# Reordering the start of a fused adaLN, linear-attention and SwiGLU kernel: the last q tile between the shift products, another order of the first norms, another bank rotation

## The chip, the cores and the metric

The kernel runs on one core of one Trainium2 chip. TensorE (PE) multiplies, VectorE (DVE) and ScalarE (ACT) work on its results and on SBUF, GpSimd (POOL) does a few small operations, and SyncE (SP) issues the DMAs. The metric is the device time of one execution in microseconds (us). The time before is 828.32 us, the median of three runs (827.97 to 828.67).

## The reference, cut to what matters

One transformer block over a sequence of 2048 tokens of width 1024, in bf16, with its norms modulated by a condition vector:

```python
def _A_ref(x, wqkv, wo):                      # linear attention, 32 heads of 32
    q, k, v = split(x @ wqkv)
    phi = lambda t: jnp.where(t > 0, t + 1, jnp.exp(t)) + 1e-06
    pq, pk = (phi(q), phi(k))
    kv = jnp.einsum('bhsd,bhse->bhde', pk, v)
    z = jnp.einsum('bhsd->bhd', pk)
    num = jnp.einsum('bhqd,bhde->bhqe', pq, kv)
    den = jnp.einsum('bhqd,bhd->bhq', pq, z)[..., None] + 1e-06
    return merge_heads(num / den) @ wo

mod = (_silu(c) @ w_mod).reshape(c.shape[0], 6, 1, -1)
sa, ca, ga, sb, cb, gb = mod                  # shift, scale and gate of each half
h = _layernorm(x, axis=-1) * (1 + ca) + sa
x = x + ga * _A_ref(h, A_wqkv, A_wo)
h = _layernorm(x, axis=-1) * (1 + cb) + sb
x = x + gb * _B_ref(h, B_w_gate, B_w_up, B_w_down)   # (silu(h@wg) * (h@wu)) @ wd, width 3584
```

The change touches only the first part: the first layer norm of tokens 0 to 1023, its modulation with `ca` and `sa`, and the q and k products of the first 512 tokens.

## The kernel before

**Order and synchronisation.** Every operation is written once, in program order, through a small recorder (`P.pe`, `P.dve`, `P.act`, `P.pool`, `P.dma`). Each engine executes its own operations strictly in that order. The recorder adds a wait wherever an operation reads or overwrites what another engine or a DMA wrote or still reads. In SBUF it follows byte ranges, so two tiles placed on the same bytes depend on each other. In PSUM it follows whole banks: when an engine touches a bank, it waits for the last operation of every other engine on that bank. All operations are recorded at line 176, so the profile tells them apart by their tiles. There is no planner; the order is written by hand.

**Tokens.** The sequence is cut into 16 tiles of 128 tokens (`st`) and 4 chunks of 512 tokens (`ch`). `XRES` holds x, `HT` holds the normalised, modulated and transposed activations of two chunks (buffer `ch % 2`), eight tiles of 128 features (`dt`) each. `WQK` holds the q and k weights.

**Start (lines 628 to 661).** Tiles 0 and 2 get their mean and variance on VectorE (`bn_stats` twice, `bn_aggr`, `ln1_rstd1`); tiles 1 and 3 get sums on ScalarE (`act_stats`), from which VectorE makes the variance (`msq_neg`, `ve_sums`). POOL raises each variance to -0.5. VectorE normalises each tile in place (`ln1_xn`, `ln1_xn_sum`), and TensorE transposes it into PSUM banks 4 to 7 (`tile_transposes`). `mod_sc` computes columns of the modulation: for each of the columns asked for, eight products with one moving column, into PSUM bank 0. `fin_ca` and `fin_sa` copy the scale (plus 1) and the shift out of bank 0. `warm` issues TensorE products on zeros, which nothing reads. `h0_first` scales a transposed `dt` tile out of PSUM into `HT`; `raw_copy` moves the last four unscaled.

**q of chunk 0 (`q_phase_chunk0`, line 773).** The q products of chunk 0 run while the weights of `w_mod` and `WQK` still arrive. Seven q tiles (`nt` 0 to 6) accumulate in banks 1, 2, 3, 4, 6, 7, 5 at once, over `dt` in passes. The first four `dt` tiles are scaled but not shifted; their shift is added as a bias per output feature. That bias is a product of the shift column and the weights (`bias_mm`), accumulated in bank 0 and copied to `BIASQ` by `bias_fin`. The eighth q tile runs last, in bank 0, after that copy:

```python
for i, dt in enumerate((4, 5, 0, 1, 2, 3, 6, 7)):
    P.pe("matmul", out=PS[:, 0, :], lhsT=WQK[:, dt, 896:1024], rhs=HT[:, 0, dt, :], ...)
```

After it `h0_shift` adds the shift to `dt` 0 to 3 for the k products. `q_phi` computes the exponential and the relu of each q tile on ScalarE with the bias; `q_min` and `q_add` finish phi on VectorE into `PQT`. In between, tiles 4 to 7 (chunk 1) are normalised and transposed by DMA from SP (`th_dma`).

**k of chunk 0 and the later chunks.** `k_group` and `q_group` compute one output tile of 128 features over a whole chunk, eight products, into a bank from `next_bank`, and `phi_evac` evicts it. A k tile takes one exponential on ScalarE into one of four slots of `E1`, then, for two tiles together, a min on VectorE and a `scalar_tensor_tensor` that reads the bank again and writes `PKT` (`phi_flush`). Side work hangs on the groups: `kside[gi]` is recorded behind group `gi` of chunk 0, and `s1`, `s2`, `s3` behind the groups of chunks 1 to 3. The modulation of chunk 1's `HT` (`th_mod`, in halves of 256 tokens: tiles 4 and 5, then 6 and 7) hangs on group 1 of chunk 0. In chunk 1 the side work is the norms of chunk 2 (groups 0 to 2), its modulation, divided between VectorE (even `dt`) and ScalarE (odd `dt`) at groups 9 to 11, and ScalarE's sums of tiles 14 and 15. Chunks run 8 k groups and 8 q groups each.

**Loads.** SP issues all loads in one order: x tiles 0 to 3, the first half of `WCA` (the scale's weights), parts of `WQK`, the second half of `WCA`, more of `WQK`, `WSA` half 1 (the shift's weights), the rest of q's `WQK`, `WSA` half 0 in two pieces, x tiles 4 and 5, k weights, x tiles 6 and 7, k weights, x tiles 8 to 11. Then come the transposing DMAs of tiles 4 to 7 and x tiles 12 to 15.

**The rest** (attention's products, output projection, SwiGLU) runs from about 126 us to the end and isn't touched.

Of the kernel before, what the change touches and what calls it, by code (L numbers as in the profile page):

```python
# [5 lines left out]
FP32 = mybir.dt.float32  # L6
# [256 lines left out]
def bass_adaLN_cond__linear_attn_block__swiglu_ffn__prompt_kernel(  # L263
# [22 lines left out]
    with ExitStack() as es:  # L286
# [6 lines left out]
        def T(name, off, shape, dt):  # L293
            n = 1
            for s_ in shape[1:]:
                n *= s_
            assert off % 32 == 0 and off + n * mybir.dt.size(dt) <= ARENA, (name, off, shape)
            return nc.alloc_sbuf_tensor_at(name, shape, dt, offset=base + off)
# [47 lines left out]
        RL = T("rl", 188 * KB, [128, 4, 512], BF16)  # L346
        E1X = T("e1x", 192 * KB, [128, 4, 512], BF16)
        RLX = T("rlx", 196 * KB, [128, 4, 512], BF16)
        ACC = T("acc", 192 * KB, [128, D], FP32)
        MHL = T("mhl", 196 * KB, [128, 2, D], BF16)  # L350
        MHLT = T("mhlt", 192 * KB, [128, 2 * NDT, 128], BF16)
# [105 lines left out]
        def warm(n=1, bank=2):  # L457
            for _ in range(n):
                P.pe("matmul", out=PS[:, bank, :], lhsT=IDENT[:], rhs=E1[:, 0, :], start=True, stop=True)
# [23 lines left out]
        def ln1_xn(st, c0=0, c1=D):  # L483
            P.dve("tensor_scalar", out=XRES[:, st, c0:c1], in0=XRES[:, st, c0:c1],
                  scalar1=MV[:, st, 0:1], scalar2=RSTD[:, st:st + 1], op0=ALU.subtract, op1=ALU.mult)
# [22 lines left out]
        def mod_sc(w, c0, ms, kts=range(NDT)):  # L508
            for m in ms:
                for kt in kts:  # L510
                    P.pe("matmul", out=PS[:, 0, c0 + m:c0 + m + 1], lhsT=w[:, kt, m * 128:(m + 1) * 128],
                         rhs=SILUC[:, kt:kt + 1], start=mod_first[0], stop=(kt == NDT - 1), skip_group_check=True)
                    mod_first[0] = False

        def fin_ca(m, n):
            P.dve("tensor_scalar", out=MODCOL[:, 0, m:m + n], in0=PS[:, 0, 8 + m:8 + m + n], scalar1=1.0, scalar2=None,
                  op0=ALU.add)

        def fin_sa(m, n, cast=False):
# [42 lines left out]
        def ln1_rstd1(st):  # L562
            P.dve("tensor_scalar", out=VE[:, st:st + 1], in0=MV[:, st, 1:2], scalar1=EPS, scalar2=None, op0=ALU.add)
            P.pool("tensor_tensor", out=RSTD[:, st:st + 1], in0=VE[:, st:st + 1], in1=NEGHALF[:, 0:1], op=ALU.pow)
# [13 lines left out]
        def act_stats(st, passes=(0, 1)):  # L578
            junk0 = HT[:, 1, 0:2, :] if st < 4 else JUNK1[:]
            for i in passes:  # L580
                fn_, sc_, acc_ = ((ACT.Identity, 1.0 / D, SUMX), (ACT.Square, D ** -0.5, SUMSQ))[i]
                P.act("activation", out=junk0, in_=XRES[:, st, :].rearrange("p (a b) -> p a b", a=2),
                      func=fn_, scale=sc_, accum_out=acc_[:, st:st + 1])
# [39 lines left out]
        def ve_sums(st):  # L623
            P.dve("tensor_scalar", out=VE[:, st:st + 1], in0=SUMSQ[:, st:st + 1], scalar1=MV[:, st, 1:2], scalar2=EPS,
                  op0=ALU.add, op1=ALU.add)
            pool_pow(st)

        warm(13, bank=3)
        act_stats(1)
        act_stats(3)  # L630
        for f in s0_:
# [1 line left out]
        ln1_rstd1(0)  # L633
        msq_neg(1)
        s2_[0]()
        ln1_xn(0)
        tile_transposes(0)
        warm(5, bank=3)
        ve_sums(1)
        s2_[1]()  # L640
        s2_[2]()
        ln1_rstd1(2)
        ln1_xn_sum(1)
        tile_transposes(1)
        warm(1, bank=3)
        msq_neg(3)
        ln1_xn(2, 0, 512)
        ve_sums(3)
        ln1_xn(2, 512, D)
        tile_transposes(2)  # L650
        mod_sc(WCA, 8, range(2))
        ln1_xn_sum(3, 0, 512)
        ln1_xn_sum(3, 512, D)
        fin_ca(0, 2)
        tile_transposes(3)
        mod_sc(WCA, 8, range(2, 4))
        h0_first(0, "dve")
        h0_first(1, "dve")
        raw_copy(4, "dve")
# [43 lines left out]
        def next_bank():  # L703
            i = qk_ctr[0]
            qk_ctr[0] += 1
            return (1, 2, 3, 4, 6, 7, 5, 0)[i % 8] if i < 40 else i % 5 + 1

        def q_group(ch, nt):
            buf, bank = ch % 2, next_bank()
# [39 lines left out]
        def mod_row_b(bank, i, dst):  # L749
# [3 lines left out]
            P.wait_for("sp", [wr])  # L753
            P.dma("mdr%d" % i, dst[:], MDR[i].unsqueeze(0).to_broadcast([128, D]))

        def q_slot(nt):
            return (E1, RL) if nt < 4 else (E1X, RLX)

        def q_phi(nt, bank):
            for buf, fn_ in zip(q_slot(nt), (ACT.Exp, ACT.Relu)):  # L760
                P.act("activation", out=buf[:, nt % 4, :], in_=PS[:, bank, :], func=fn_, bias=BIASQ[:, nt:nt + 1])

        def q_min(nts):
            for nt in nts:
                e = q_slot(nt)[0][:, nt % 4, :]
                P.dve("tensor_scalar", out=e, in0=e, scalar1=1.0, scalar2=1e-6, op0=ALU.min, op1=ALU.add)

        def q_add(nts):
            for nt in nts:
                e, r = q_slot(nt)  # L770
                P.dve("tensor_tensor", out=PQT[:, nt, 0:512], in0=r[:, nt % 4, :], in1=e[:, nt % 4, :], op=ALU.add)

        def q_phase_chunk0():
            qb = [1, 2, 3, 4, 6, 7, 5]
            fin_ca(2, 2)
            for dt in (2, 3):
                h0_first(dt, "dve")
            for nts, dts in ((range(3), (0,)), (range(3), (1,)), ((3, 4, 5, 6), (0, 1))):
                for nt in nts:
                    q_part(nt, qb[nt], dts)  # L780
            for nt in range(7):
                if nt == 4:
                    mod_sc(WCA, 8, range(4, 8))
                    fin_ca(4, 4)
                    for dt in (4, 5):
                        h0_scale_only(dt)
                q_part(nt, qb[nt], (2, 3))
            act_stats(4, (0,))
            for nt in range(7):
                if nt == 6:  # L790
                    mod_sc(WSA, 0, range(6, 8))
                    fin_sa(6, 2)
                    for dt in (6, 7):
                        h0_scale(dt)
                q_part(nt, qb[nt], (4, 5))
            mod_sc(WSA, 0, range(4, 6))
            fin_sa(4, 2, True)
            for dt in (4, 5):
                h0_shift(dt)
            for nt in range(7):  # L800
                if nt == 2:
                    bias_mm((4, 5))
                q_part(nt, qb[nt], (6,))
            for nt in range(7):
                if nt == 1:
                    mod_sc(WSA, 0, range(4), range(4))
                if nt == 3:
                    mod_sc(WSA, 0, range(4), range(4, 8))
                    fin_sa(0, 4, True)
                    ln_ops[1][0]()  # L810
                if nt == 5:
                    bias_mm(range(4))
                    bias_fin()
                q_part(nt, qb[nt], (7,))
            ln_ops[1][1]()
            ln_ops[1][2]()
            ln1_rstd1(5)
            for i, dt in enumerate((4, 5, 0, 1, 2, 3, 6, 7)):
                P.pe("matmul", out=PS[:, 0, :], lhsT=WQK[:, dt, 896:1024], rhs=HT[:, 0, dt, :], start=(i == 0),
                     stop=(i == 7))  # L820
            for dt in range(4):
                h0_shift(dt)
            ln1_xn(5)
            th_dma(5)
            for nt in range(2):
                q_phi(nt, qb[nt])
            act_stats(4, (1,))
            for nt in range(2, 8):
                q_phi(nt, qb[nt] if nt < 7 else 0)
            for f in ln_ops[2]:  # L830
                f()
            act_var(4)
            pool_pow(4)
            for f in ln_ops[3]:
                f()
            ln1_rstd2(6)
            ln1_xn_sum(4)
            th_dma(4)
            q_min((0, 1))
            for st in (6, 7):  # L840
                ln1_xn(st)
                th_dma(st)
            q_add((0, 1))
            for nts in ((2, 3), (4, 5)):
                q_min(nts)
                q_add(nts)
            qk_ctr[0] = 0

        def add(d, k, f):
# [2 lines left out]
        kside = {}  # L852
        ln_ops = [ln1_stats_ops(4 + jj) for jj in range(4)]

        for c0 in (0, 256):
            for dt in range(NDT):
                add(kside, 1, lambda dt=dt, c0=c0: th_mod(1, dt, c0, c0 + 256))
        add(kside, 1, lambda: q_min((6, 7)))
        add(kside, 1, lambda: q_add((6, 7)))
        for jj, k in ((0, 3), (1, 4)):  # L860
            add(kside, k, lambda jj=jj: act_stats(10 + jj))
        q_phase_chunk0()
        for st in range(12, 16):
# [384 lines left out]
```

## Time and profile before

| what | value |
|---|---|
| median of three runs | 828.32 us (827.97 to 828.67) |
| the profiled execution | 827.71 us |
| its span, first to last instruction | 826.0 us |
| granted TensorE clock | 1.000 |
| TensorE matmul busy | 816.3 us, 99% |
| VectorE busy | 312.2 us, 38% |
| ScalarE busy | 197.0 us, 24% |

The busy time of a stretch, by engine (us):

| stretch | PE | DVE | ACT | POOL |
|---|---|---|---|---|
| 0 to 10 | 7.51 | 6.89 | 6.06 | 3.06 |
| 10 to 15 | 4.78 | 3.22 | 2.52 | 0.24 |
| 30 to 40 | 9.95 | 9.30 | 10.00 | 1.48 |
| 40 to 50 | 9.95 | 10.00 | 7.68 | 0.00 |
| 50 to 60 | 9.95 | 9.75 | 3.13 | 2.16 |
| 60 to 72 | 11.95 | 10.14 | 11.52 | 0.81 |

In a line of the timeline the first number is the start in us from the first instruction, the second the length, then engine, line, operation, the tile written and the tiles read, the shape and the number of instructions merged; in brackets stands the idle time of the engine before it and what ended it. PEld is TensorE's weight load, which runs ahead of the product; SPq is SP's queue while it issues a DMA. A line of a wait has the total in us, the number of waits and the longest. A line of a DMA issue ends with the us from the issue to the landing. Over the whole kernel VectorE is busy 38% of the time, but between 30 and 62 us it hardly stops.

### The profile page before, as it was taken

The numbers are of one execution on the slowest core, as the hardware profiler recorded it, in microseconds if no ns is written. First come the engines' busy times: TensorE is split into PE (matmuls) and PEld (weight loads), VectorE is DVE, ScalarE is ACT, GpSimd is POOL, SyncE is SP. The second block draws the span as 40 slices with busy tenths as digits, with TensorE's granted clock in tenths as the row PEclk, the third lists the DMA queues.
The fourth block names the chain that finished last, engine by engine and source line by source line (L and its number), as shares of the span: only waits on it lengthen the run. The fifth ranks groups of instructions, "written<-read, shape, count | busy, mean of one in ns | idle before, by whom it ended". The sixth has DMA issues, their size and how long they took to land.

```text
span 826.0 us, 10436 instructions
## 1 busy us (share of the span) xinstructions
PE 816.3 (99%) x4243; PEld 375.9 (46%) x4322; DVE 312.2 (38%) x672; ACT 197.0 (24%) x338; POOL 41.0 (5%) x58
## 2 busy tenths in 40 slices
PE   8999999999999999999999999999999999999998
PEld 4544444444444444444444444444444444444444
DVE  5798988477945521111221112122111111221111
ACT  4758642123341111011111101111110111111011
POOL 1110000000130000020000003000000300000000
DMA  9969756865698995600455570045557004553000
GB/s 316 297 139 223 167 159 149 181 175 211 149 253 245 296 249 153 166 26 26 136 151 151 153 174 25 23 131 153 151 152 182 27 19 126 151 152 88 0 26 26
DMA packets 199392, 119.32 MB, mean 144 GB/s; under 512 B 58024, under 2 KB 183088, under 8 KB 199344
## 3 DMA queue, kind: packets, MB, share of 16 engines
q1 hardware_dynamic: 199328, 118.65, 53.8%
q8 instruction: 34, 0.56, 0.3%
q14 instruction: 14, 0.11, 0.0%
q10 hardware_dynamic: 16, 0.00, 0.0%
HBM read 100.67 MB, written 4.33 MB: 127 GB/s over the span
## 4 chain that ended last, share of the span: by engine, by line
PE 98%; issue 1%; DMA 0%; DVE 0%; POOL 0%; SPq 0%
PE ps L176 98%; DMA xres<-in_A_x_dram 0%; POOL rstd L176 0%; DVE xres L176 0%; DVE stats L176 0%; SPq L176 0%; DVE ht L176 0%; DVE ve L176 0%; DVE mv L176 0%; DVE modcol L176 0%
## 5 line engine op out<-in xcount | busy, mean ns | idle before, releaser
L176 PE MATMUL ps<-h2t,gug 128*128 128x512 bf16 x878 | 210.1, 379 | 0.9
L176 PE MATMUL ps<-h2t,guu 128*128 128x512 bf16 x878 | 209.9, 379 | 0.9
L176 DVE TENSOR_TENSOR at<-sg,ps 128x512 bf16<-128x512 bf16 x112 | 77.0, 687 | 282.8 <-PE ps L176 270.6
L176 ACT ACTIVATE sg<-ps 128x512 bf16<-128x512 f32 x112 | 66.9, 597 | 309.7 <-PE ps L176 298.3
L176 PEld LDWEIGHTS ps<-h2t,guu 128*128 128x128 bf16 x896 | 87.7, 98 | 105.7
L176 PEld LDWEIGHTS ps<-h2t,gug 128*128 128x128 bf16 x896 | 87.6, 98 | 105.5
L176 PE MATMUL ps<-wd_a,at 128*128 128x512 bf16 (+1 forms) x502 | 111.9, 377 | 0.5
L176 PE MATMUL ps<-ht,wqk 128*128 128x512 bf16 x499 | 110.7, 379 | 0.9 <-DVE ht L176 0.2
L176 PE MATMUL ps<-wd_b,at 128*128 128x512 bf16 (+1 forms) x377 | 84.6, 377 | 0.4
L176 PEld LDWEIGHTS ps<-wd_a,at 128*128 128x128 bf16 x512 | 50.1, 98 | 59.6
L176 DVE TENSOR_TENSOR ut<-att,gb_b 128x512 bf16<-128x512 bf16 (+1 forms) x32 | 13.6, 426 | 167.5 <-ACT att L176 167.5
L176 PEld LDWEIGHTS ps<-ht,wqk 128*128 128x128 bf16 x512 | 49.2, 98 | 58.9 <-DVE ht L176 1.0
L176 ACT ACTIVATE att<-ps 128x512 bf16<-128x512 f32 (+1 forms) x32 | 17.4, 591 | 182.1 <-PE ps L176 182.1
L176 PEld LDWEIGHTS ps<-wd_b,at 128*128 128x128 bf16 x384 | 37.6, 98 | 44.7
L176 PE MATMUL ps<-pk,xres 128*128 128x512 bf16 x250 | 55.4, 379 | 0.6 <-issue 0.5
L176 PE MATMUL ps<-mw,pqt 128*128 128x512 bf16 x249 | 55.4, 379 | 0.5 <-issue 0.2
L176 POOL TENSOR_SCALAR h2t<-h2t,modcol 128x512 bf16<-128x512 bf16 x32 | 26.5, 846 | 383.0 <-DMA h2t<-xn 383.0
L176 ACT ACTIVATE e<-ps 128x512 bf16<-128x512 f32 x56 | 33.3, 611 | 31.8 <-PE ps L176 15.8
L176 ACT ACTIVATE junk<-xres 128x1024 bf16<-128x1024 bf16 x26 | 27.6, 1063 | 45.9 <-DVE xres L176 34.2
L176 PEld LDWEIGHTS ps<-mw,pqt 128*128 128x128 bf16 x256 | 24.8, 98 | 30.0 <-issue 0.5
L176 PEld LDWEIGHTS ps<-pk,xres 128*128 128x128 bf16 x256 | 24.6, 98 | 30.1 <-issue 1.3
L176 DVE SCALAR_TENSOR_TENSOR xres<-ps,xres 128x512 bf16<-128x512 f32 x32 | 21.5, 688 | 11.6 <-PE ps L176 11.3
(111 smaller groups left out, 337.8 us busy)
## 6 DMA issues: line engine op xcount, KB each, us to landing
gug<-in_B_w_gate_dram SPq DMA_DIRECT2D x56, 512.0 KB, 4.0
guu<-in_B_w_up_dram SPq DMA_DIRECT2D x56, 512.0 KB, 5.3
xres<-in_A_x_dram SPq DMA_DIRECT2D x20, 256.0 KB, 4.4
rb<-recip_den SPq DMA_DIRECT2D x8, 512.0 KB, 11.7
stgx<-in_w_mod_dram SPq DMA_DIRECT2D x2, 2048.0 KB, 9.3
wd_a<-in_B_w_down_dram SPq DMA_DIRECT2D x4, 1024.0 KB, 7.7
out_dram<-xres SPq DMA_DIRECT2D x31, 128.0 KB, 1.7
xres<-in_A_x_dram SPq DMA_DIRECT2D x3, 1024.0 KB, 6.5
```

What stands on the lines that cost most here:

```text
L176: return getattr(e, method)(**kw)
```

## The change

- **Start.** Tile 2's statistics on VectorE (both halves, then the aggregate) and tile 1's variance move ahead of tile 0's norm. TensorE issues 18 warm-up products ahead of the first transposes instead of 13, and none between the transposes (six before). Three columns of the scale instead of two come ahead of tile 3's transposes, and one instead of two behind them; `fin_ca` copies three and one.
- **Last q tile.** Its eight products move from behind the bias to between the shift products, in the order `dt` 0 to 7, into the bank of q tile 0. ScalarE first copies q tile 0 from that bank, as soon as it is complete, into a new fp32 tile `QRAW` (at 202 KB, on the second half of `PKT[0]`). The pass over `dt` 7 runs through all seven tiles without shift products between them.
- **phi of q.** The order is tile 1 to 7 and then 0, and tile 0 is read from `QRAW`; the slots follow that order.
- **ScalarE.** The sums of x tile 4 move behind the copy to `QRAW`, both together; before, one was ahead of the `dt` 4 and 5 pass and the other between the first phis.
- **VectorE.** Half of tile 5's statistics stands ahead of the shift's copy. Tile 4's variance moves ahead of the bias copy, and its norm and transposing DMA ahead of tile 5's. The last four q tiles' min and add move behind k tiles 2 and 3; two pairs are finished before the k tiles instead of three. The first halves of chunk 1's modulation move ahead of k tiles 0 and 1.
- **Rotation.** Chunk 0's k groups, chunk 1 and chunk 2 take the banks in another order; bank 1 comes back after six groups twice and after five once, and bank 5 after five once, where they came back after five to eight before.
- **Side work.** ScalarE's sums of tiles 10 and 11 come one group later.

```diff
+        QRAW = T("qraw", 202 * KB, [128, 512], FP32)
...
-        warm(13, bank=3)
+        warm(18, bank=3)
         act_stats(1)
         act_stats(3)
...
         s2_[0]()
+        s2_[1]()
+        ve_sums(1)
+        s2_[2]()
+        ln1_rstd1(2)
         ln1_xn(0)
         tile_transposes(0)
-        warm(5, bank=3)
-        ve_sums(1)
-        s2_[1]()
-        s2_[2]()
-        ln1_rstd1(2)
         ln1_xn_sum(1)
         tile_transposes(1)
-        warm(1, bank=3)
...
-        mod_sc(WCA, 8, range(2))
+        mod_sc(WCA, 8, range(3))
...
-        fin_ca(0, 2)
+        fin_ca(0, 3)
         tile_transposes(3)
-        mod_sc(WCA, 8, range(2, 4))
+        mod_sc(WCA, 8, range(3, 4))
...
-            return (1, 2, 3, 4, 6, 7, 5, 0)[i % 8] if i < 40 else i % 5 + 1
+            if i < 24:
+                return (0, 2, 3, 4, 6, 7, 5, 1)[i % 8]
+            if i < 40:
+                return (0, 2, 3, 4, 6, 1, 7, 5, 0, 2, 3, 1, 4, 6, 7, 5)[i - 24]
+            return i % 5 + 1
...
+        QORD = (1, 2, 3, 4, 5, 6, 7, 0)
+
         def q_slot(nt):
-            return (E1, RL) if nt < 4 else (E1X, RLX)
+            i = QORD.index(nt)
+            bufs = (E1, RL) if i < 4 else (E1X, RLX)
+            return [t[:, i % 4, :] for t in bufs]
...
+        def q_pair(i):
+            q_min(QORD[i:i + 2])
+            q_add(QORD[i:i + 2])
...
-            act_stats(4, (0,))
...
             for nt in range(7):
-                if nt == 1:
+                q_part(nt, qb[nt], (7,))
+                if nt == 0:
+                    P.act("activation", out=QRAW[:], in_=PS[:, qb[0], :], func=ACT.Copy)
+                    act_stats(4)
+            for i, dt in enumerate(range(NDT)):
+                if i == 1:
                     mod_sc(WSA, 0, range(4), range(4))
-                if nt == 3:
+                if i == 3:
                     mod_sc(WSA, 0, range(4), range(4, 8))
+                    ln_ops[1][0]()
                     fin_sa(0, 4, True)
-                    ln_ops[1][0]()
-                if nt == 5:
+                    ln_ops[1][1]()
+                    act_var(4)
+                    pool_pow(4)
+                if i == 5:
                     bias_mm(range(4))
                     bias_fin()
-                q_part(nt, qb[nt], (7,))
-            ln_ops[1][1]()
+                P.pe("matmul", out=PS[:, qb[0], :], lhsT=WQK[:, dt, 896:1024], rhs=HT[:, 0, dt, :], start=(i == 0),
+                     stop=(i == 7))
             ln_ops[1][2]()
             ln1_rstd1(5)
-            for i, dt in enumerate((4, 5, 0, 1, 2, 3, 6, 7)):
-                P.pe("matmul", out=PS[:, 0, :], lhsT=WQK[:, dt, 896:1024], rhs=HT[:, 0, dt, :], start=(i == 0),
-                     stop=(i == 7))
             for dt in range(4):
                 h0_shift(dt)
+            ln1_xn_sum(4)
+            th_dma(4)
             ln1_xn(5)
             th_dma(5)
-            for nt in range(2):
-                q_phi(nt, qb[nt])
-            act_stats(4, (1,))
-            for nt in range(2, 8):
-                q_phi(nt, qb[nt] if nt < 7 else 0)
+            for nt in QORD:
+                q_phi(nt, QRAW[:] if nt == 0 else PS[:, qb[nt % 7], :])
             for f in ln_ops[2]:
                 f()
-            act_var(4)
-            pool_pow(4)
             for f in ln_ops[3]:
                 f()
             ln1_rstd2(6)
-            ln1_xn_sum(4)
-            th_dma(4)
-            q_min((0, 1))
+            q_min(QORD[0:2])
             for st in (6, 7):
                 ln1_xn(st)
                 th_dma(st)
-            q_add((0, 1))
-            for nts in ((2, 3), (4, 5)):
-                q_min(nts)
-                q_add(nts)
+            q_add(QORD[0:2])
+            q_pair(2)
+            for dt in range(NDT):
+                th_mod(1, dt, 0, 256)
             qk_ctr[0] = 0
...
-        for c0 in (0, 256):
-            for dt in range(NDT):
-                add(kside, 1, lambda dt=dt, c0=c0: th_mod(1, dt, c0, c0 + 256))
-        add(kside, 1, lambda: q_min((6, 7)))
-        add(kside, 1, lambda: q_add((6, 7)))
-        for jj, k in ((0, 3), (1, 4)):
+        for dt in range(NDT):
+            add(kside, 1, lambda dt=dt: th_mod(1, dt, 256, 512))
+        for i in (4, 6):
+            add(kside, 3, lambda i=i: q_pair(i))
+        for jj, k in ((0, 4), (1, 5)):
             add(kside, k, lambda jj=jj: act_stats(10 + jj))
```

More of the change, by code (lines that the diff above doesn't have):

```diff
@@ L754, in mod_row_b, with q_phi @@
             P.dma("mdr%d" % i, dst[:], MDR[i].unsqueeze(0).to_broadcast([128, D]))
+        QORD = (1, 2, 3, 4, 5, 6, 7, 0)
         def q_slot(nt):
-            return (E1, RL) if nt < 4 else (E1X, RLX)
-        def q_phi(nt, bank):
+            i = QORD.index(nt)
+            bufs = (E1, RL) if i < 4 else (E1X, RLX)
+            return [t[:, i % 4, :] for t in bufs]
+        def q_phi(nt, src):
             for buf, fn_ in zip(q_slot(nt), (ACT.Exp, ACT.Relu)):
-                P.act("activation", out=buf[:, nt % 4, :], in_=PS[:, bank, :], func=fn_, bias=BIASQ[:, nt:nt + 1])
+                P.act("activation", out=buf, in_=src, func=fn_, bias=BIASQ[:, nt:nt + 1])
         def q_min(nts):
             for nt in nts:
-                e = q_slot(nt)[0][:, nt % 4, :]
+                e = q_slot(nt)[0]
                 P.dve("tensor_scalar", out=e, in0=e, scalar1=1.0, scalar2=1e-6, op0=ALU.min, op1=ALU.add)
@@ L770, in q_add @@
                 e, r = q_slot(nt)
-                P.dve("tensor_tensor", out=PQT[:, nt, 0:512], in0=r[:, nt % 4, :], in1=e[:, nt % 4, :], op=ALU.add)
+                P.dve("tensor_tensor", out=PQT[:, nt, 0:512], in0=r, in1=e, op=ALU.add)
+        def q_pair(i):
+            q_min(QORD[i:i + 2])
+            q_add(QORD[i:i + 2])
         def q_phase_chunk0():
             qb = [1, 2, 3, 4, 6, 7, 5]
-            fin_ca(2, 2)
+            fin_ca(3, 1)
             for dt in (2, 3):
```

## The prediction

> **What bounds the kernel now.** First the page's chain of work that ended last, then the waits of TensorE's weight loads from 28 to 112 us.
>
> ```profile
> span 826.0 us, 10436 instructions
> ...
> PE 98%; issue 1%; DMA 0%; DVE 0%; POOL 0%; SPq 0%
> ```
> ```profile
> PEld ps L176 <- DVE ht L176: 1.0, 6, 0.2
> PEld ps L176 <- DVE pkt L176: 0.5, 1, 0.5
> ```
>
> TensorE (PE) is the path. From the first q product at 11.8 us to 112 us it stands only where a weight load waits: six short ones at 43.4 to 44.7 and one at 46.75, where matmuls lose about 0.2 us in all. So a gain can only be an earlier first q product and those 0.2 us; a loss is a new wait. Next the timeline of the start, VectorE (DVE) alone: what the first product waits for.
>
> ```profile
> 6.39 0.53 DVE L176 TENSOR_SCALAR xres<-xres,mv,rstd 128x1024 bf16<-128x1024 bf16 x1
> ...
> 8.97 0.41 DVE L176 TENSOR_SCALAR xres<-xres,mv,rstd 128x512 bf16<-128x512 bf16 x1 [0.32 <-POOL rstd L176]
> 9.30 0.21 DVE L176 TENSOR_SCALAR ve<-sumsq,mv 128x1 f32<-128x1 f32 x1
> ...
> 10.27 0.73 DVE L176 TENSOR_SCALAR xres<-xres,sumx,rstd 128x512 bf16<-128x512 bf16 x2 [0.44 <-POOL rstd L176]
> ```
>
> The reader is to see VectorE waiting twice for a power on POOL: 0.32 us before tile 2's norm, 0.44 us before tile 3's. Then the two engines behind TensorE, where the result will be made: VectorE has no idle worth naming from 39 to 62 us, ScalarE (ACT) none from 60.9 to 74 us.
>
> ```profile
> 40.43 4.18 DVE L176 TENSOR_SCALAR ht<-ht,modcol 128x256 bf16<-128x256 bf16 x16
> ```
> ```profile
> 50.48 1.28 DVE L176 BATCH_NORM_STATS2 stats<-xres 128x6 f32<-128x512 bf16 x2
> ```
> ```profile
> 60.86 0.60 ACT L176 ACTIVATE e<-ps 128x512 bf16<-128x512 f32 x1 [0.42 <-DVE pkt L176]
> ...
> 70.57 1.52 ACT L176 ACTIVATE ht<-ht,modcol 128x512 bf16<-128x512 bf16 x2
> 71.98 0.60 ACT L176 ACTIVATE e<-ps 128x512 bf16<-128x512 f32 x1
> ```
>
> ScalarE's stretch starts at 60.86 when VectorE frees a buffer, and its last modulation of chunk 2's `HT` ends at 72.10. TensorE, 14 groups of 1.726 us after 46.75, starts chunk 2 at 70.92 and wants that tile (dt 7) at 72.43. With 0.06 us for the signal the slack is 0.28 us. That is the number to remember. Last, SP's timeline and the DMA issues, for the transposing DMAs of chunk 1's tiles 5 and 4:
>
> ```profile
> 30.12 2.77 SPq L176 DMA_TRANSPOSE ht<-xres  x1
> ...
> 34.07 2.22 SPq L176 DMA_TRANSPOSE ht<-xres  x1
> ```
> ```profile
> ht<-xres SPq DMA_TRANSPOSE x1, 7.3
> ...
> ht<-xres SPq DMA_TRANSPOSE x1, 4.2
> ```
>
> They land at 37.4 and 38.3: the first queued behind the x loads (the last issued at 29.02, landed 7.4 later, 36.4), the second 0.9 after the first.
>
> **The change, part by part.**
>
> *Start, VectorE.* Tile 2's second sum and tile 1's variance go ahead of tile 0's norm; no work is added. Tile 0's norm moves from 6.39 to about 7.44 and ends 7.97. TensorE's 18 warm-ups (13 end at 6.92; five more by 0.216) end at 8.00, so nothing is exposed; six later ones are gone. POOL's two powers (0.57 to 0.78 each) run back to back from 7.28 and end between 8.45 and 8.9, against 8.94. Tile 2's norm can so start 0 to 0.45 earlier, but tile 3's variance needs ScalarE's last sum, which ends 8.97: it starts at 9.00 at best, against 9.30. Gain at tile 3's norm: 0 to 0.3; I take 0.27.
>
> *Start, TensorE.* Eight of the 32 one-column products move from behind tile 3's transposes to ahead of them: 8 x 0.025 = 0.20 us. They wait for the first `WCA` half (issue 2.65, 7.2 to landing: 9.83). So 24 run from 9.9 to 10.5, the transposes from 10.5 (10.74 before), the last eight products take 0.2 instead of 0.4. The first scaled tile comes by VectorE: `fin_ca` after the 24th column at 10.69, the scale 10.90 to 11.39, product at 11.44 instead of 11.77: 0.33 earlier, between 0 and 0.45. The loads allow it: second `WCA` half 15.6 (wanted 16.2), `WSA` half 1 20.5 (wanted 20.7).
>
> *The last q tile.* Its eight products go from behind the bias to between the shift products, into bank 1. Same TensorE work. New: ScalarE copies bank 1 to `QRAW`, 0.6 to 0.7 us (rows of 512-column fp32 evictions, 0.58 to 0.79), starting 0.42 after that bank's last product is issued; with 0.1 for the signal 1.2 us, and TensorE comes back after 7 x 0.2157 = 1.51. Hidden by 0.3. Behind the copy ScalarE holds tile 4's two sums: x lands 25.5, they end 27.9, the first phi needs the bias at 28.7. Hidden. On VectorE a half sum of tile 5 (x lands 26.2, 0.69 long) now stands ahead of the shift's cast, which is due at 27.2: hidden by 0.2.
> The bias, however, is finished later: seven more products precede it (1.51 us), less the 0.33 gained, so 27.33 becomes 28.51. All of VectorE's work behind it starts 0.47 us late (28.59 against 28.13 for tile 5's aggregate; the half sum no longer stands between).
>
> *VectorE to 50 us.* From 28.59, by the same rows: variance 0.32, four shifts 1.05, norms of 4 and 5 0.91, sums and aggregates of 6 and 7 3.0, then a wait for POOL (power 0.93; tile 4's norm no longer fills it, so 0.73 instead of 0.28), norms 0.91, four min and four add. VectorE reaches the first-half modulations at 37.75. Before, 16 modulations stood behind k tiles 0 and 1; now eight stand ahead, so a new wait: for the landing of tiles 4 and 5. Behind it in VectorE's queue stand k tiles 0 and 1, and behind these TensorE's banks and `HT`.
> That landing, L, is not in the trace, since the two issues move: SP issues tile 4 at about 30.5 and tile 5 when the first issue ends, 33.4. Lower bound, by the shortest issue-to-landing: 33.4 + 4.2 = 37.6. Upper, by the longest: 33.4 + 7.3 = 40.7. I take 38.3: the nearest rows are the same two transfers, behind the same loads, and the second is ready in time to follow the first as before.
> From L + 0.03: eight modulations 2.05, two k tiles 1.62, eight modulations 2.05, two k tiles 1.62, four min and add 2.15, four k tiles 3.25: 12.75, so VectorE starts chunk 2's statistics at L + 12.78 = 51.1, against 50.48. Lag 0.6.
> TensorE meets nothing before that: chunk 1 starts 42.79 (43.12 before), its dt 0 is modulated at 42.3, dt 7 at 44.2 (wanted 44.3). The k banks come 0.7 us or more in time, and the wait at 46.75 is gone.
>
> *ScalarE to 72 us.* No idle separates VectorE's 50.48 from 60.86, and none follows on ScalarE, so its last modulation also ends 0.6 late, 72.7 + 0.06. TensorE, 0.51 ahead by then (0.33 and the 0.18 us), wants it at 71.92: it stands 0.85 us. Net: lag 0.61 - slack 0.28 = **+0.33 us**, whatever the start gained. In general L - 37.97, and not under -0.22, where VectorE rather than the landing sets it.
>
> *Bank rotation.* Banks 1 and 5 return after five or six groups instead of eight, 8.6 us at least; the slowest eviction of the rows there (chunk 1's last q tile: group ends 70.9, relu 76.0) takes 5.1. Nothing.
>
> Sum: the profiled run's 827.71 (span 826.0 and 1.71 around it) becomes 828.04. It stood 0.61 under the median of 828.32, so the forecast is 828.32 + 0.33 = 828.65, said as **828.6 us**.
>
> **One rule against the change.** In the trace the first eight warm-ups come every 0.427 us, the rest every 0.216 from 5.7 us on; between the last warm-up (ends 9.26) and 11.77 only transposes and one-column products run, 2.5 us, and the next product is still fast. After the change that stretch is 8.0 to 11.44, 3.4 us. The Trainium skill (TensorE: Matmul & The Clock Gate, Part 1: The HAM clock gate) says that an idle window of about 3.4 us halves the clock again, and its Part 4, PE-mode transpose, that transposes don't count as busy in the same way; no run here shows 3.4 us. By it the sum is rival 3's; by the row, nothing.
>
> **The rivals.**
> 1. *Faster: tiles 4 and 5 land by 37.7.* For it: both are ready earlier than the second was (34.07), and 4.2 us from 33.4 is 37.6. Against: the loads before them are unchanged. Then VectorE goes on at 37.75, its lag is 0.06, and 0.06 - 0.28 = -0.22: 828.1.
> 2. *Slower, the other side: they land late.* VectorE stands at the first modulation with k tiles 0 and 1 behind it; each us costs a us. For it: the transfer ahead took 7.3 us, 40.7 by that, +2.7 or 831.0. It decides (over 0.2%) from L = 39.6. Against: 7.3 was the wait behind loads that are through by 36.4.
> 3. *The clock falls at 11.4.* Slow until as much work has run as at the start, 3.1 us at half pace: TensorE 1.5 late, VectorE's 37.75 becomes 39.3, lag 1.56 - 0.28 = +1.3: 829.6. For it only the longer stretch; against it the 2.5 us that passed, with 1.8 us of transposes in it.
> 4. *The reordering gains nothing* (the `WCA` landing and the 24 columns hold the transposes): VectorE reaches 38.1, still before L, so +0.33 again. It changes no number.
>
> **How the numbers follow.** Likeliest, L within 37.9 to 38.8: 0.62, own range 828.2 to 829.2. Rival 1: 0.24. Rival 2 beyond 39.6: 0.05, and L between 38.8 and 39.6: 0.04. Rival 3: 0.03. A front gain that survives whole because ScalarE's chain gives way, -0.5 (827.8): 0.02. Runs of this kernel differ by 0.35 around the median, so 827.8 to 829.8 leaves out under 2 in 10. 0.2% (1.66 us) is about what a measurement can tell from no change: faster than 826.66 has no mechanism, 0.02; slower than 829.98 is rival 2 (0.05) and the upper half of rival 3, 0.07; 0.91 lies within.
>
> **What would show it.** First q product near 11.4. Bias copy near 28.5. First modulation (128x256) on VectorE near 38.3 with a DMA wait of some 0.6 before it; chunk 2's statistics near 51.1. No weight-load wait at 43 to 47, and a new one of about 0.8 us for ScalarE's `HT` at 71 to 73. Wrong if VectorE doesn't wait at 38, if ScalarE idles between 61 and 72, or if the first q products come every 0.43 us.

## The result, and the profile after

| | before | after |
|---|---|---|
| median of 22 runs each | 828.15 us (827.62 to 829.23) | 830.05 us (827.64 to 831.20) |
| ratio, 95% interval | | 1.0017 (1.0011 to 1.0023) |
| the profiled execution, its span | 827.71, 826.0 us | 829.07, 827.3 us |
| first q weight load, us from the start | 11.74 | 12.33 |
| copy of the bias | 27.33 | 29.44 |
| landing of tile 5's transposing DMA | (second of the pair: 38.3) | 38.60 |
| first weight load of chunk 3 | 98.35 | 99.04 |

The changed kernel is a little slower: 0.17% by the ratio, which the means of the runs give too (829.70 to 828.26); the medians lie 0.23% apart. That is just inside the 0.2% that was called no change, but 1 lies outside the interval, which reaches 0.23%. The median is 1.45 us above the 828.6 forecast and 0.25 above the range; the ratio, applied to the 828.32 that the forecast started from, makes 829.7, just within it. The spread is the second result: before stays within 1.6 us, after takes 3.6 us, with six runs up to 828.71, the profiled one at 829.07, and 15 from 829.73 on. The one profile of it, at 829.07, lies between the two.

The page's header and chain of work of after:

```profile
span 827.3 us, 10514 instructions
...
PE 99%; ACT 0%; issue 0%; DMA 0%; DVE 0%; ACTq 0%
```

The waits of TensorE's weight loads of after, 28 to 112 us:

```profile
PEld ps L176 <- ACT ht L176: 0.8, 2, 0.5
PEld ps L176 <- DVE modcol L176: 0.4, 1, 0.4
```

The seven waits at 43 to 47 us are gone, and a wait of 0.8 us for ScalarE's `HT` has come, as forecast. The other line is the shift's cast ahead of the bias, at 28.4 us, which before had at 26.3 too; it is only moved into this window.

The start, on TensorE's weight loads. In order: the timeline of before, then that of after.

```profile
5.57 1.02 PEld L176 LDWEIGHTS ps<-e,ident 128*128 128x128 bf16 x5 [0.28 <-issue]
...
11.74 0.34 PEld L176 LDWEIGHTS ps<-ht,wqk 128*128 128x128 bf16 x3
```
```profile
8.06 1.01 PEld L176 LDWEIGHTS ps<-e,ident 128*128 128x128 bf16 x5 [0.28 <-issue]
9.19 1.54 PEld L176 LDWEIGHTS ps<-ident,xres 128*128 128x128 bf16 x24
10.69 0.71 PEld L176 LDWEIGHTS ps<-siluc,wca 128*128 128x128 bf16 x24
...
12.33 0.56 PEld L176 LDWEIGHTS ps<-ht,wqk 128*128 128x128 bf16 x4 [0.29 <-issue]
```

The merged x5 is the point from which the warm-ups run at full pace: 5.57 us in this execution of before, 8.06 in that of after. The 18 warm-ups therefore end past 9 us, not at 8.00, and hold up the transposes, although VectorE had the first tile ready at 8.0 (its timeline of after):

```profile
7.47 0.54 DVE L176 TENSOR_SCALAR xres<-xres,mv,rstd 128x1024 bf16<-128x1024 bf16 x1
...
9.24 0.40 DVE L176 TENSOR_SCALAR xres<-xres,mv,rstd 128x512 bf16<-128x512 bf16 x1
10.09 0.73 DVE L176 TENSOR_SCALAR xres<-xres,sumx,rstd 128x512 bf16<-128x512 bf16 x2 [0.44 <-POOL rstd L176]
```

Next the two engines behind TensorE: VectorE's first-half modulations and chunk 2's statistics, and ScalarE's last modulations for chunk 2, all in the timeline of after.

```profile
38.70 2.15 DVE L176 TENSOR_SCALAR ht<-ht,modcol 128x256 bf16<-128x256 bf16 x8 [0.24 <-DMA ht<-xres]
...
51.45 1.30 DVE L176 BATCH_NORM_STATS2 stats<-xres 128x6 f32<-128x512 bf16 x2
```
```profile
61.84 0.60 ACT L176 ACTIVATE e<-ps 128x512 bf16<-128x512 f32 x1 [0.42 <-DVE pkt L176]
...
71.55 1.52 ACT L176 ACTIVATE ht<-ht,modcol 128x512 bf16<-128x512 bf16 x2
```

VectorE waits for the DMA, the statistics start 0.97 us later than before (50.48), ScalarE ends 0.97 later (73.07 against 72.10), and chunk 3 starts 0.69 later. Its first weight load, in the timeline of before and then of after:

```profile
98.35 0.10 PEld L176 LDWEIGHTS ps<-ht,wqk 128*128 128x128 bf16 x1
```
```profile
99.04 0.10 PEld L176 LDWEIGHTS ps<-ht,wqk 128*128 128x128 bf16 x1
```

SP's issue of tile 5's transposing DMA in after, and its time to landing (the last number of the DMA row):

```profile
33.27 3.34 SPq L176 DMA_TRANSPOSE ht<-xres  x1
```
```profile
ht<-xres SPq DMA_TRANSPOSE x1, 5.3
```

A second loss, of 0.70 us, lies far from the change. In the g products TensorE stands 1.07 us where it stood 0.38 before. In order: after, then before.

```profile
174.24 0.76 PEld L176 LDWEIGHTS ps<-pk,xres 128*128 128x128 bf16 x5 [1.07 <-issue]
```
```profile
172.66 0.33 PEld L176 LDWEIGHTS ps<-pk,xres 128*128 128x128 bf16 x3 [0.38 <-issue]
```

In after VectorE's first scaling of P starts at 163.05, when the reciprocals land (161.28 before), as its timeline shows:

```profile
163.05 1.23 DVE L176 TENSOR_TENSOR pqt<-pqt,rb 128x2048 bf16<-128x2048 bf16 x1 [7.73 <-DMA rb<-recip_den]
```

So 0.69 + 0.70 account, within 0.03, for the 1.36 us between the two profiled executions. They don't account for the 15 runs above 829.7, which the experiments had to find.

### The profile page after: what moved, and what is told of

It reads as the page before. It is cut to its first block, busy times and chain, and to the rows that moved or that the text cites. A ratio compares the mean times of both kernels' runs of the same rounds, so it can differ in the third digit from the quotient of the medians.

```text
span 827.3 us, 10514 instructions
## 1 busy us (share of the span) xinstructions
PE 821.4 (99%) x4321; PEld 376.3 (45%) x4321; DVE 313.4 (38%) x672; ACT 197.6 (24%) x339; POOL 40.6 (5%) x58
## 4 chain that ended last, share of the span: by engine, by line
PE 99%; ACT 0%; issue 0%; DMA 0%; DVE 0%; ACTq 0%
PE ps L176 99%; DMA cs<-in_c_dram 0%; ACT ht L176 0%; ACT e L176 0%; ACT rl L176 0%; DVE ht L176 0%; DVE xres L176 0%; ACT junk L176 0%; ACTq L247 0%
## 5 line engine op out<-in xcount | busy, mean ns | idle before, releaser
L176 PEld LDWEIGHTS ps<-wd_b,at 128*128 128x128 bf16 x384 | 37.6, 98 | 44.7
L176 POOL TENSOR_SCALAR h2t<-h2t,modcol 128x512 bf16<-128x512 bf16 x32 | 26.3, 837 | 383.0 <-DMA h2t<-xn 383.0
```

Source lines behind the costliest of these rows:

```text
L176: return getattr(e, method)(**kw)
```

## The experiments

All medians are against the runs of before on the same chip: 828.22 us for the first four kernels, 828.18 for the next four, 828.32 for the last four.

### One half of the change at a time

The start alone, on the kernel before:

```diff
-        warm(13, bank=3)
+        warm(18, bank=3)
...
+        s2_[1](); ve_sums(1); s2_[2](); ln1_rstd1(2)
         ln1_xn(0)
         tile_transposes(0)
-        warm(5, bank=3)
-        ve_sums(1); s2_[1](); s2_[2](); ln1_rstd1(2)
...
-        mod_sc(WCA, 8, range(2))
+        mod_sc(WCA, 8, range(3))
```

> Only the start of the change (lines 628 to 656 with 18 warm-ups ahead of the transposes, three scale columns first); the q phase is the one of before. Theory 1 (the loss is a lag of VectorE and ScalarE that the q phase makes, by the later bias): no lag here, -0.3 to +0.1 us against before. Theory 2 (the loss is made by 18 warm-ups that run at the slow pace of 0.427 us for as long as the clock has not been released and hold the transposes): +0.7 to +1.5 us, with the spread of the changed kernel (over 3 us) instead of that of before (1.6 us).

Measured: 827.84 us (827.75 to 828.72), ratio 0.9999 (0.9990 to 1.0008). At the median the start costs nothing, and gains nothing either. In its profile the first q weight load is at 11.84, and the timeline of the weight loads says what holds it:

```profile
10.24 0.66 PEld L176 LDWEIGHTS ps<-siluc,wca 128*128 128x128 bf16 x24 [0.29 <-DMA wca<-in_w_mod_dram]
```

The one-column products wait for `WCA` to land, so VectorE's earlier norms bring TensorE nothing.

The other half: everything else of the change, with the start of before (the diff above taken back from after).

> Only the q phase and the rotation of the change, with the start of before (13, 5 and 1 warm-ups). Theory 1: +1.2 to +1.9 us against before, as the whole change. Theory 2: 0 to +0.4 us.

Measured: 830.08 us (827.95 to 831.00), ratio 1.0019 (1.0010 to 1.0027): the whole loss and the whole spread. The cause is in the q phase or behind it.

### Warm-ups, and the place of the first-half modulations

The changed kernel with as many warm-ups as before:

```diff
-        warm(18, bank=3)
+        warm(13, bank=3)
```

> The changed kernel with 13 warm-ups instead of 18 ahead of the transposes, nothing else. Theory 1: within 0.3 us of the changed kernel, so +1.1 to +1.9 against before. Theory 2: five slow warm-ups fewer are up to 2.1 us at the start, the time falls to within 0.5 us of before and the spread narrows.

Measured: 828.54 us (827.72 to 829.27), ratio 1.0005 (0.9996 to 1.0014). By the number this speaks for the start as the cause, which the two runs above exclude. In its profile tile 5 lands at 38.45, and no run of it lies above 829.3. Why thirteen warm-ups keep it out of the upper group here, and thirteen in the kernel of the second run do not, stays open.

The changed kernel with the first-half modulations behind k tiles 0 and 1 again:

```diff
             q_pair(2)
-            for dt in range(NDT):
-                th_mod(1, dt, 0, 256)
...
-        for dt in range(NDT):
-            add(kside, 1, lambda dt=dt: th_mod(1, dt, 256, 512))
+        for c0 in (0, 256):
+            for dt in range(NDT):
+                add(kside, 1, lambda dt=dt, c0=c0: th_mod(1, dt, c0, c0 + 256))
```

> The changed kernel with the first halves of chunk 1's modulation put back behind k tiles 0 and 1. VectorE then does not wait for the landing of tiles 4 and 5 but for ScalarE's exponentials of k tiles 0 and 1, which stand behind the q phis and end at 39.6 and 40.1 in the trace. Theory 1: 16 modulations follow, VectorE reaches chunk 2's statistics 1.0 to 1.3 us later than in the changed kernel and TensorE waits at 43 to 45: +0.7 to +1.3 us against the changed kernel. Theory 2: no difference to the changed kernel (under 0.3 us).

Measured: 829.00 us (828.76 to 829.60), ratio 1.0010 (1.0002 to 1.0019). Neither theory said this: the median is lower than that of after, and the runs lie within 0.84 us. Its profile held the clue. Tile 5 landed at 40.31, 1.7 us later than in after, and VectorE did not wait for it, as its timeline shows (no bracket):

```profile
40.96 2.14 DVE L176 TENSOR_SCALAR ht<-ht,modcol 128x256 bf16<-128x256 bf16 x8
```

### The two later places

The next theory (3) put the spread down to the wait at 174 us. Four kernels take out the later places. The scaling of P one group later, on after and on before:

```diff
-            if 7 <= g < 15:
-                scale_pq(g - 7)
-            if g == 10:
+            if 8 <= g < 16:
+                scale_pq(g - 8)
+            if g == 11:
                 P.dma("stgx1", STGX[0][:], wmv[:, :, 3072:4096])
```

> The changed kernel with each scaling of P by the reciprocals one group of g products later (and the staging load that follows it). Theory 1 (all of the loss comes from ScalarE's modulations for chunk 2, +.7 us in the profile of after): nothing changes, about +1.2 to +1.9 us against before, as after. Theory 3 (a second loss sits at the g products at about 172 to 174 us, where VectorE stands at the first scaling until the reciprocals land, and it comes and goes with the execution): the median falls to +.3 to +.9 against before, the runs within 1.5 us of each other, and no gap of over .5 us on the weight loads between 165 and 180 us.

> The same step alone on the kernel before. Theory 1: 0. Theory 3: the reciprocals land at 161.3 us there as the scaling starts (161.28), so the gap of .375 us on the weight loads at 172.7 goes at most: 0 to -.4 us; a loss above .3 us would say that the later scaling has a price of its own, to be taken off the run above.

Two of ScalarE's modulations for chunk 2 moved to VectorE, and then both steps together:

```diff
-            if dt % 2 == 0 or ch == 1:
+            if dt % 2 == 0 or ch == 1 or (ch == 2 and dt > 4):
                 P.dve("tensor_scalar", out=HT[:, buf, dt, c0:c1], ...)
```

> The changed kernel with two of ScalarE's four modulations for chunk 2 (dt 5 and 7) on VectorE. Theory 1: the wait of .8 us at 72.4 to 73.1 goes, so -.6 to -.8 against after in every run, and the median comes to +.4 to +1 against before, most of what is left unexplained. Theory 3: the same .7 at chunk 3, but the runs keep their two groups, 1 to 2 us apart, since the chain of the reciprocals is as late as before against the products; the median moves by less than .5 or more than 1, as the groups fall.

> The changed kernel with both steps. Theory 1: as the run with the chunk 2 step alone. Theory 3: both losses go, 0 to -.4 us against before, the runs within 1.2 us of each other.

| kernel | median (range), us | ratio (95%) | runs above 829.5 |
|---|---|---|---|
| after, scaling later | 828.69 (827.55 to 830.82) | 1.0009 (1.0000 to 1.0018) | 5 of 11 |
| before, scaling later | 828.07 (827.48 to 828.69) | 0.9995 (0.9986 to 1.0003) | 0 of 11 |
| after, chunk 2 shared | 829.72 (828.08 to 830.48) | 1.0010 (1.0001 to 1.0019) | 6 of 11 |
| after, both | 829.81 (828.10 to 830.73) | 1.0016 (1.0007 to 1.0025) | 8 of 11 |

Theory 3 falls: with both places treated the runs still spread over 2.6 us and the median stays 1.6 above before. Theory 1, in its form of a fixed 0.7 us, falls too: the two groups remain. Sharing chunk 2 only moves the wait to VectorE: in that profile ScalarE's `HT` is waited for no more, VectorE's 0.4 us. But the profile of the changed kernel with the scaling later was taken of an execution from the upper group, 829.99 us. The waits of its weight loads, 28 to 112 us:

```profile
PEld ps L176 <- DVE ht L176: 2.5, 8, 1.4
PEld ps L176 <- ACT ht L176: 1.4, 2, 1.0
```

Its VectorE timeline, and its DMA row for tile 5, issued at 33.17:

```profile
40.37 2.14 DVE L176 TENSOR_SCALAR ht<-ht,modcol 128x256 bf16<-128x256 bf16 x8 [2.21 <-DMA ht<-xres]
```
```profile
ht<-xres SPq DMA_TRANSPOSE x1, 7.1
```

Issued 0.1 us earlier than in after, the same transfer lands at 40.28 instead of 38.60. VectorE stands 2.21 us with k tiles 0 and 1 behind it. That is rival 2 of the prediction. What delays the landing is seen in the DMA view, 33 to 43 us, each digit and each GB/s figure 0.25 us. In order: after, then this kernel.

```profile
DMA  9999999879411179999999999980006999999797
GB/s 385 361 389 370 308 308 189 128 113 71 62 49 46 35 174 289 279 291 289 265 216 202 208 260 168 90 5 8 9 9 146 287 218 293 420 377 352 229 303 295
```
```profile
DMA  9999999891111199999999900000899999961899
GB/s 369 377 349 350 286 226 148 130 80 49 49 57 31 38 281 280 283 293 292 291 211 179 26 0 2 7 10 9 175 289 276 280 252 206 172 57 74 295 328 385
```

Both have a pause with under 30 GB/s, of 1.0 and 1.5 us. In after it starts at 39.5, when tile 5 has landed (38.60); here it starts at 38.5, ahead of tile 5's end.

The DMA queues between the landings of tiles 4 and 5 show what else is there. In order: after (37.72 to 38.60), then this kernel (37.62 to 40.28). A line gives the queue, the kind, the packets, the MB, and the packets' time as a share of the span of 16 engines.

```profile
q1 hardware_dynamic: 813, 0.20, 112.9%
```
```profile
q1 hardware_dynamic: 1039, 0.26, 114.9%
q8 instruction: 1, 0.02, 3.3%
```

One 16 KB packet of the kind `instruction` starts at 37.84 here, while tile 5 is under way. In after it starts at 38.87, 0.27 us behind tile 5's landing. The kernel with the modulations put back, where tile 5 landed at 40.31, has it at 38.11, again ahead of the landing. No run moved this packet, so its part is read from fourteen profiles and not tried (see the last section).

### The landing, moved on purpose

Theory 4: the landing L sets the loss, because the change took its cover away. The same dose in both kernels tests it, and the opposite dose. First, in after, x tiles 8 to 11 behind the transposing DMAs instead of ahead:

```diff
-        for st in range(8, 12):
-            x_load(st)
...
         q_phase_chunk0()
-        for st in range(12, 16):
+        for st in range(8, 16):
             x_load(st)
```

> The changed kernel with the loads of x tiles 8 to 11 queued behind the four transposing DMAs of tiles 4 to 7 instead of ahead of them. Theory 4 (the landing L of tile 5's transposing DMA sets the loss: L - 37.97 us at chunk 3; it lands at 38.1 to 38.9 us in some executions and at 40.3 in others, 40.28 in the 829.99 us execution of the run with the later scalings): L comes to 37 to 38 us in every execution, the chunk 2 wait falls to 0 to .2 us, and the median to -.3 to +.5 against before, the slow group gone. Theory 5 (the loss is the start: eighteen warm-ups under a clock that is let go late, 12.0 to 12.6 us for the first q weight load instead of 11.74): nothing changes, +1 to +1.9.

Second and third, two more x tiles ahead of them, in after and in before:

```diff
-        for st in range(8, 12):
+        for st in range(8, 14):
             x_load(st)
...
-        for st in range(12, 16):
+        for st in range(14, 16):
             x_load(st)
```

> The changed kernel with the loads of x tiles 12 and 13 queued ahead of those DMAs too, two more tiles of .65 us each. Theory 4: L moves by 1.3 us, to 39.9 us or more, and the median to +2 to +3.5 against before. Theory 5: as the changed kernel, +1 to +1.9.

> The same two loads ahead in the kernel before, whose modulations of tiles 4 and 5 start at 40.43 us behind the first two k tiles. Theory 4: a landing at 39.6 us (38.3 + 1.3) is covered there, 0 to +.4; where the landing slips further, to 41.6, at most +1. If it loses as much as the changed kernel does by the same step, the cover is not what differs and theory 4 falls. Theory 5: 0.

Fourth, the first edit with 13 warm-ups and the later scaling of P:

> The changed kernel with the loads behind (as the first of these), thirteen warm-ups as before, and the scalings of P one group later: all three losses named so far are taken out. Theory 4: -.6 to +.1 us against before. Theory 5: as the run with thirteen warm-ups alone, +.1 to +.6.

| kernel | median (range), us | ratio (95%) | L in the profile |
|---|---|---|---|
| after, loads behind | 828.48 (827.53 to 830.49) | 1.0001 (0.9992 to 1.0010) | 35.64 |
| after, two more loads ahead | 831.41 (830.28 to 831.96) | 1.0033 (1.0020 to 1.0045) | 41.99 |
| before, two more loads ahead | 829.16 (828.43 to 830.12) | 1.0010 (1.0002 to 1.0019) | 41.69 |
| after, loads behind, 13 warm-ups, scaling later | 828.23 (827.55 to 830.41) | 0.9999 (0.9991 to 1.0008) | 36.19 |

VectorE's first modulations in three of them, each from its timeline. In order: after with the loads behind, after with two more ahead, before with two more ahead.

```profile
37.88 2.13 DVE L176 TENSOR_SCALAR ht<-ht,modcol 128x256 bf16<-128x256 bf16 x8
```
```profile
42.09 1.12 DVE L176 TENSOR_SCALAR ht<-ht,modcol 128x256 bf16<-128x256 bf16 x4 [4.06 <-DMA ht<-xres]
```
```profile
41.79 1.37 DVE L176 TENSOR_SCALAR ht<-ht,modcol 128x256 bf16<-128x256 bf16 x5 [0.58 <-DMA ht<-xres]
```

And the waits of TensorE's weight loads for VectorE's `HT`, 28 to 112 us: after with two more ahead, then before with two more ahead.

```profile
PEld ps L176 <- DVE ht L176: 4.3, 8, 3.2
```
```profile
PEld ps L176 <- DVE ht L176: 1.9, 8, 0.7
```

With this step the changed kernel stands 3.1 us above before (five runs), and the kernel before 0.8 above itself. In the latter's profile, 1.37 us late at chunk 3, 0.71 of that is there already at the first q weight load (12.45 instead of 11.74); in the former's, 4.08 late at chunk 3, it is 0.16 (11.90). Against its own median the changed kernel rises by 1.4; 15 of its 22 runs already lay in the upper group without this step. With almost the same landing VectorE waits 4.06 us in one and 0.58 in the other: the cover, two k tiles ahead of the modulations, is what differs.

With the landing early 9 of 11 runs lie below 829.0, and with 13 warm-ups and the later scaling 10 of 11 below 829.2, as the runs of before do (827.57 to 829.38). The other three, 829.71, 830.49 and 830.41, are the only runs of these two kernels with a mean granted clock of 0.998 instead of 1.000. An estimate from that: 0.002 x 828 is about 1.7 us of full clock lost, and they stand 1.3 to 2.3 us above the medians of the rest. Where in the execution the clock was lower isn't recorded, since they were not profiled. So among the runs at full clock the upper group is gone, as theory 4 had it. Two of its numbers were missed: L came to 35.64 and not to 37 to 38, and the wait at chunk 2 stayed at 0.8 us instead of 0 to 0.2.

Theory 5 falls as the cause of the two groups: under it neither step could have moved the changed kernel. A smaller share of the loss is the start's, as the next section shows.

No kernel is shown to beat the one before: the lowest ratio, 0.9995, has 1 in its interval.

## Why the prediction was right, and where it was wrong

The mechanism was right, and so was the side of the 0.2%. The time was wrong, because one term, L, was given as a value around 38.3 with 0.09 for everything beyond 38.8.

**The formula held.** The prediction had chunk 2's statistics at L + 12.78 and the net loss at L - 37.97, whatever the start gains. Where VectorE waits for the landing, the profiles measured it over 3.5 us of L:

| profile | L | statistics: L + 12.78, measured | net: L - 37.97, chunk 3 against 98.35 |
|---|---|---|---|
| after, 13 warm-ups | 38.45 | 51.23, 51.47 | 0.48, 0.71 |
| after | 38.60 | 51.38, 51.45 | 0.63, 0.69 |
| after, scaling later | 40.28 | 53.06, 53.14 | 2.31, 2.36 |
| after, two more loads ahead | 41.99 | 54.77, 54.84 | 4.02, 4.08 |

"Whatever the start gained" holds only there. In four profiles VectorE comes later than the landing, 26.05 us after the first q weight load, and chunk 3 follows that:

| profile | L | first q weight load | first modulation | chunk 3 against 98.35 |
|---|---|---|---|---|
| after, loads behind | 35.64 | 11.82 | 37.88 | 0.19 |
| the change without its start | 38.08 | 12.25 | 38.30 | 0.32 |
| after, chunk 2 shared | 38.16 | 12.29 | 38.34 | 0.45 |
| after, loads behind, 13 warm-ups, scaling later | 36.19 | 12.43 | 38.48 | 1.17 |

So a late start costs time when the landing is early. In the last row it doesn't explain all: VectorE also waits there for tile 7's landing (0.16 us) and for ScalarE (0.19), and the rest is open.

**Step that failed: "I take 38.3", and rival 2's chance of 0.05.** Both bounds, 37.6 and 40.7, held with these loads, but the landings seen are two: 38.1 to 38.9, and 40.3. An L of 40.3 makes 2.3 us, so 828.15 + 2.3 = 830.5, in the middle of the 15 runs of after from 829.73 to 831.20. That those runs had the late landing is argued from this sum, from the profiled execution of 829.99 us and from the runs with the landing moved; their own landings were not recorded. Two things on record support it. Of the six profiles of changed kernels with these loads and the modulations ahead, the five at 829.07 or below land at 38.1 to 38.9, and the one at 829.99 at 40.28. And 14 of the 15 runs have a granted clock of 1.000, so that a lower clock isn't what they share. The prediction took before's single profile as the rule for the pair ("the second is ready in time to follow the first as before"). In before a late landing up to 40.43 costs nothing, so its time could not show it.

**The start: gain of 0.33 taken, none measured.** Two things failed. The warm-ups "end at 8.00, nothing exposed" took the moment of full pace (5.57) from one execution. In the fourteen profiles it lies between 5.6 and 8.8 us. The first q weight load lies between 11.74 and 12.45 with the start of before, and between 11.72 and 12.60 with the changed one. The Trainium skill (TensorE: Matmul & The Clock Gate, Part 1: The HAM clock gate) says that the number of slow products is run-variable, since the window that the gate watches runs freely; the traces agree, with 7 to 14 products of 0.427 us. And rival 4, the landing of `WCA`, holds the rest, as the run of the start alone showed.

**The bias copy**: 28.51 forecast, 29.44 measured. The seven products' 1.51 held exactly: 27.33 + 1.51 + 0.59 from the later start makes 29.43. VectorE reached the modulations at 38.46 instead of 37.75, by most of the same delay, which left it only 0.24 of wait. So in the profiled execution an early landing would have saved little: by the prediction's own sum 38.46 + 12.75 - 50.48 - 0.28 = 0.45 of the 0.69 would have stayed.

**The waits**: those at 43 to 47 went, and the one at 72 to 73 came, 0.8 us where 0.85 was forecast. The net of 0.33 became 0.69 in the profiled execution, since L was 38.60 and the start late.

**Rival 1** (early landing, 828.1) was tried: with L at 35.64 VectorE is the bound, as forecast, but the net is +0.19 and not -0.22. VectorE comes at 37.88 and meets 0.19 of idle for ScalarE on the way; statistics start at 50.96 against 50.48.

**Rival 3** isn't in any profile: in that of after the first q products follow at 0.215 us after 3.2 us with only transposes and one-column products. But five runs of changed kernels show a granted clock of 0.998: the three named above, one of the 22 of after (830.35) and one with chunk 2 shared (829.75). None of the 93 runs of before whose clock is listed does. They may be rival 3; where their clock fell isn't recorded.

**Not foreseen**: the 0.70 us at 174 us. It is in the profile of after alone: in the thirteen others this gap is 0.57 us at most, within 0.2 of before's 0.38. Moving the scaling by one group is not shown to cure it: on before it gave 0.9995 with 1 in the interval.

## What to carry to other kernels

Work that waits for a DMA and is moved ahead of other work loses the cover of that other work: ask not only when the transfer landed in the trace, but how late it may land in any execution, and price the late case with the formula of the path. Where before hides a variation, its profile and its spread can't show it; move the landing on purpose by a load or two in both kernels, and the cover can be measured. A spread that grows is a result in itself, and one profile of a kernel whose runs fall into two groups explains only its own group.

## What the runs showed of the hardware that was not expected

- The same transposing DMA, issued at 33.2 or 33.3 us behind the same loads, took 5.3 us to land in one execution and 7.1 in another. In each of the fourteen profiles one 16 KB `instruction` packet of 0.9 to 1.4 us starts between 37.8 and 39.8 us, and 0.4 to 0.9 us behind its start comes a pause of 1.0 to 1.5 us in which the DMA engines move under 30 GB/s. In four profiles the packet starts ahead of the landing of the pair's second transfer, which then takes 6.85 to 7.10 us; in the other ten it starts behind that landing, and the transfer takes 3.2 to 5.3 us. That the packet makes the pause is inferred from this order. What sets its time, 25.8 to 27.9 us after the first q weight load, stays open.
- The full clock can hold while only transposes and one-column products run. With 13 warm-ups, all of them slow (0.427 us each), the weight loads of the transposes turn fast after the first. The timeline of the changed kernel with 13 warm-ups:

```profile
7.28 0.15 PEld L176 LDWEIGHTS ps<-e,ident 128*128 128x128 bf16 x1 [0.27 <-issue]
7.73 0.13 PEld L176 LDWEIGHTS ps<-ident,xres 128*128 128x128 bf16 x1 [0.29 <-DVE xres L176]
8.13 1.17 PEld L176 LDWEIGHTS ps<-ident,xres 128*128 128x128 bf16 x19 [0.28 <-issue]
```

  From 8.4 us on these transposes follow each other at 0.056 us, and the first q products at 11.96 at 0.215: the clock stayed up for 3.5 us of transposes, 32 one-column products and the gaps between them. The Trainium skill (TensorE: Matmul & The Clock Gate, Part 4: PE-mode transpose) says that the full clock does not engage for transposes; in this profile it held among them. Whether they could have released it isn't shown: the last warm-up product started at 7.70, 0.43 us ahead of the first transpose.
